# Attention and a feed-forward layer in one kernel: x buffers moved, weight copies issued later, a block's accumulators taken in another order

## The chip, the cores and the metric

The kernel runs on one core of a Trainium2 chip. A core has TensorE (PE in the profile, its weight loads PEld), VectorE (DVE), ScalarE (ACT), GpSimd (POOL), and SyncE (SP), which here only issues DMAs; 16 DMA engines move the data. The metric is the device time of one execution in microseconds, lower is better. Times of several runs are given as their median.

## The reference

Banded causal attention, then a feed-forward layer with a gate. All inputs and outputs are float32. Batch 8, 8 heads, 576 positions, head size 64; the feed-forward layer has 4608 tokens, width 512 and inner width 2048.

```python
scores = scale * np.matmul(q, k.transpose(0, 1, 3, 2))
rel = pos[:, None] - pos[None, :]
scores = np.where((rel >= 0) & (rel < 64), scores, -1000000000.0)
scores = scores - np.max(scores, axis=-1, keepdims=True)
attn = np.exp(scores)
attn = attn / (np.sum(attn, axis=-1, keepdims=True) + 1e-09)
x = np.matmul(attn, v)                       # to (4608, 512): tokens by heads x head size
h = x @ w_in
g = np.where(h >= 1, h, np.where(h <= -1, 0.0, (h + 1) ** 2 / 4.0))
return (g @ w_out).astype(np.float32)
```

## The kernel before, in words

**Precision.** Matrix products of the feed-forward layer are done in float32r, a form in which TensorE takes 32-bit operands. Each operand is split into a high part and the rest (`xh` and `xl` of x, `gh` and `gl` of the gate, two parts of each weight), and a product is three matmuls: high by high, high by rest, rest by high.

**Tiles.** The 4608 tokens are nine tiles of 512. The inner width is cut in 16 pieces f of 128. For the first three tiles ("plain", t = 0, 1, 2) `ffn_in` (L892) multiplies x by a piece of `w_in`, twelve matmuls of 512 columns (or two lots of 256 for the first pieces of tiles 0 and 1), the gate is worked out by ScalarE, VectorE and GpSimd (`ffn_relu`, `ffn_square`, `ffn_gate`, `ffn_high`, `ffn_low`, L906 to L933), and `ffn_out` (L938) multiplies it by a piece of `w_out` into four accumulators of one PSUM bank each, three matmuls for each 128 tokens. After the sixteenth piece `ffn_take` copies an accumulator to SBUF and `ffn_store` sends it to DRAM.

**Supers.** The other six tiles are three pairs, "supers" u = 0, 1, 2. A pair's first products are made by a scheme with seven products in place of eight: `add_products` (L857) and `ffn_product` (L824, matmuls at L831) take sums and differences of x (`x_op`, built by `add_build`) and sums and differences of weights. The moving operand of L831 is one of these x operands: some are stored in two buffers of the pool of x (called `xs` in the profile), the others in slots that weights had held (called `wts`). The halves of a super are its two tiles: `add_half(u, 0, ...)` runs the first, `add_half(u, 1, ...)` the second, each with its 16 gates and `ffn_out` (L950) into the same four accumulators, whose copies (`ffn_take`, at L274 or L276) free them.

**Weights.** They are loaded, decoded and split while tile 0 runs. Then `add_sums` (L781) prepares eight blocks of them for the supers: for block n, `sum_pass` (L739) copies three parts as they are to a DRAM buffer `kept` (three DMAs, L742), and for each half c `sum_whole` and `sum_sums` (L752 to L764) make sums in the small buffer `u`, `sum_high` and `sum_low` split them (the high parts go to a buffer of the pool `o`, which tile stores use too), and `sum_keep` (L774) stores both to `kept`. `ring_load` (L808) brings all parts back during the supers.

**Order.** Nothing is ordered by hand alone: `Plan` (L114) holds every piece of work with a key (its due place), costs by engine, what it comes after, and which buffers it takes and gives back. `run` simulates the engines with these costs and issues on each engine, among what could start soonest, the work with the lowest key; it also picks between engines where a piece may run on several. That order is then each engine's order on the chip, where instructions of one engine run strictly in order and wait only for the data and buffers that they need. What a piece "comes after" in the plan alone orders it and makes no wait on the chip. SP is one more engine of this plan, and all loads and stores but the first two are on its queue. The accumulators are the pool `acc` (4), the gate's parts `gh` and `gl` have two buffers each, `o` has two.

**Memory.** Pools lie behind one another in SBUF in the order of their opening: `const` (with `idt`, `msk`, `nmsk`, `idr`, `mskr`, `ptd`), `xpool` (x and its operands), `ld` (loads of q, k, v), `att` (`sm`, `nm`, `den`), `ffn` (`u`, `a`, `gh`, `gl`, `o`), `wpool` (weights).

Of the kernel before, what the change touches and what calls it, by code (L numbers as in the profile page):

```python
# [10 lines left out]
F32 = mybir.dt.float32  # L11
F32R = mybir.dt.float32r
# [8 lines left out]
P = 128  # L21
QB = 64
SB = 2 * QB
WIN = 128
WINDOW = 64
SQ = 32
NEAR = WINDOW + SQ
# [34 lines left out]
O_LAG_DMA = 2300  # L62
# [32 lines left out]
O_LATER = 1.5  # L95
# [11 lines left out]
SPILLED = 6  # L107
L_DVE = 4, 6, 8
G_LEAD = 1
H_LOAD = 1400  # L110
H_LEAD = 3.5


class Plan:  # L114
# [9 lines left out]
    def add(self, key, cost, do, after=(), takes=(), gives=(), lag=0, shared=False):  # L124
        self.work.append((key, cost, do, set(after), takes, gives, lag, shared))
        return len(self.work) - 1
# [75 lines left out]
def banded_attention_then_ffn(ctx: ExitStack, tc: tile.TileContext, q, k, v, w, masks, out, dims):  # L202
    nc = tc.nc
    B, H, S, D = dims
    NT, DM = out.shape
    NP = H // 2
# [3 lines left out]
    scale = 1.0 / float(D) ** 0.5  # L210
    TMAX = max(TILES)

    const = ctx.enter_context(tc.tile_pool(name="const", bufs=1))
    xpool = ctx.enter_context(tc.tile_pool(name="xpool", bufs=1))
    ld = ctx.enter_context(tc.tile_pool(name="ld", bufs=2))
    att = ctx.enter_context(tc.tile_pool(name="att", bufs=4))
# [12 lines left out]
    idt = const.tile([P, P], F32, name="idt")  # L229
    make_identity(nc, idt)  # L230
    msk = const.tile([P, 3, WIN], F32, name="msk")
    nmsk = const.tile([P, 3, WIN], F32, name="nmsk")
    idr = const.tile([P, P], F32R, name="idr")
    mskr = const.tile([P, 3, WIN], F32R, name="mskr")
    wpool = ctx.enter_context(tc.tile_pool(name="wpool", bufs=1))
    dram = ctx.enter_context(tc.tile_pool(name="dram", bufs=1, space=bass.MemoryType.DRAM))
    kept = [dram.tile([P, 7, 2, 2, P], F32, name=f"kept{n}") for n in range(NF // 2)]
# [3 lines left out]
    for n, at in ((P, QB), (QB, 0)):  # L241
# [4 lines left out]
            out=m, in_=m, compare_op=ALU.is_ge, fill=NEG, base=at - 1, pattern=[[1, WIN]], channel_multiplier=-1  # L246
        )
        nc.gpsimd.affine_select(
            out=m, in_=m, compare_op=ALU.is_ge, fill=NEG, base=WINDOW - at, pattern=[[-1, WIN]], channel_multiplier=1
# [19 lines left out]
    add = plan.add  # L269
# [127 lines left out]
        nc.sync.dma_start(out=t, in_=v[b * QB:b * QB + WIN])  # L397

    def load_masks():
        nc.sync.dma_start(out=nmsk[:, :, :NEAR], in_=masks)  # L400

    def round_masks():
        nc.scalar.copy(idr, idt)
        nc.scalar.mul(mskr[:, :2], msk[:, :2], 1.0 / scale)

    def att_scores(s, masked, pool):
        qt, kt = qts.pop(s), kts.pop(s)
        banks = [banks_of_heads(pool) for _ in range(2)]
        if masked:
            m = mskr[:, variant(s), :].unsqueeze(1).broadcast_to([P, NP, WIN])  # L410
            for ps in banks:
                nc.tensor.matmul(ps.rearrange("p a n -> p (a n)"), lhsT=idr, rhs=m, start=True, stop=False)
        m, n = (SQ, NEAR) if near(s) else (QB, WIN)
        for p in range(NP):
            for i in range(SB // m):
                r = slice(i * m, (i + 1) * m)
                for h in range(2):
                    nc.tensor.matmul(  # L418
                        banks[h][r, p, :n], lhsT=qt[half[h], p, r], rhs=kt[half[h], p, i * m:i * m + n],
                        start=not masked, stop=not masked or p == NP - 1,  # L420
                    )
        sm = att.tile([P, 2 * NP * WIN], F32, name="sm", bufs=BUFS["sm"])[:, :2 * NP * n]
        sm = sm.rearrange("p (h a n) -> p h a n", h=2, n=n)
        nm, den = (att.tile([P, 2, NP], F32, name=n, bufs=2) for n in ("nm", "den"))
        for h in range(2):
            blk[s, h] = banks[h][:, :, :n], sm[:, h], nm[:, h], den[:, h]
        blk[s, BOTH] = None, sm, nm, den
# [311 lines left out]
    def sum_pass(n):  # L739
        f0, f1 = by_chunk(n)  # L740
        for o, w_, e in (0, f0, 0), (5, f0, 1), (6, f1, 1):
            nc.sync.dma_start(  # L742
                out=kept[n][:, o].rearrange("p a c n -> p (a c) n"),
                in_=w_[:, :, :, e].bitcast(F32).rearrange("p a c n -> p (a c) n"),
            )
# [30 lines left out]
        nc.sync.dma_start(out=k[:, 1:5, 0, c], in_=half_of.pop((n, c)))  # L776
        nc.sync.dma_start(out=k[:, 1:5, 1, c], in_=sum_block(n, c))

    l1, sums_read, sums_kept, sum_last = {}, {}, {}, []

    def add_sums(n):  # L781
        key = step(1) + S_PACE * n + (S_LATE if n < 2 else S_LATER)
        ready = [w_ready[2 * n, 0], w_ready[2 * n + 1, 0], w_ready[NF - 1, 0], w_ready[NF - 1, 1]]
        xp = add(key, dict(SP=2000), lambda e: sum_pass(n), ready, lag=O_LAG_DMA)
        reads, keeps = [xp], [xp]
        for c in range(2):
            k = key + c * S_PACE / 2
            xs = add(
                k, tt(2 * P), lambda e, c=c: sum_whole(n, c, 0, e), ready + sum_last,
                takes=["tmp"] if sum_first else ["tmp", "u"], shared=True,  # L790
            )
            if not sum_first:
                sum_first.append(xs)
            x0 = add(k, tt(2 * P), lambda e, c=c: sum_whole(n, c, 1, e), [xs], shared=True)
            reads.append(x0)
            sum_last[:] = [xs]
            x = x0
            for j in range(4):
                x = add(k, tt(P), lambda e, c=c, j=j: sum_sums(n, c, j, e), [x], shared=True)
            xh = add(k, dict(ACT=90 + .84 * 4 * P), lambda e, c=c: sum_high(n, c, e), [x], takes=["o"])  # L800
            x = add(k, tt(4 * P), lambda e, c=c: sum_low(n, c, e), [xh], shared=True)
            x = add(k, dict(SP=750), lambda e, c=c: sum_keep(n, c), [x], lag=O_LAG_DMA, gives=[("tmp", xs), ("o", xh)])
            keeps.append(x)
        sums_read[n], sums_kept[n] = reads, keeps
# [219 lines left out]
    def add_stores(t, key, first, x_out):  # L1024
        end_tile, at_h, xh, sh = t == len(TILES) - 1, t >= PLAIN and (t - PLAIN) % 2 == 0, None, []
        for i in range(TILES[t] // P):
            pool = "sm" if end_tile and i < BUFS["sm"] else "hA1" if at_h and i > 1 else "o"
            xp, needs = xh if pool == "hA1" else None, [x_out[i]] + ([xh] if pool == "hA1" and xh else [])
            for n in pieces(t, i):
                m, end = n.stop - n.start, n.stop == DM  # L1030
                xo = add(
                    key + i * end_tile, dict(DVE=65 + m * 1.05, ACT=60 + m * .83), lambda e, i=i, n=n, pool=pool: ffn_take(t, i, n, e, pool),
                    needs, takes=[] if xp else [pool], gives=[("acc", *first[i])] * end,
                )
                xp = xo if xp is None else xp
                needs = [x_out[i], xo]
                xs = add(
                    key, dict(SP=790), lambda e, i=i, n=n: ffn_store(t, i, n), [xo, *sh], lag=O_LAG_DMA,
                    gives=[(pool, xp)] * (end and not (pool == "hA1" and i == 2)),
                )  # L1040
            if pool == "hA1":
                xh, sh = xp, [xs]
        return xh

    def add_ffn(t):
# [33 lines left out]
    def add_half(u, b, done, back):  # L1079
        t = PLAIN + 2 * u + b  # L1080
        r = slice(0, TILES[t])
        first, x_out, over = {}, {}, []
        for q in range(NF):
            f = (q + 2 * SPILLED * b) % NF
            n, e = f // 2, f % 2
            if b:
                key = step(PLAIN + 2 * u) + C_STEP * NF / 2 + Q_STEP * q
                key, lag = key - G_LEAD, O_LATER + G_LEAD
                split = Q_STEP / 4
            else:  # L1090
                key = step(t) + C_STEP * (n + (3 + 3 * e) / 7)
                lag = O_AFTER - C_STEP * (3 + 3 * e) / 7 + e * C_STEP / 2
                split = C_STEP / 8

            h_at[t, f] = int(back[n][e][0][2]), back[n][e][1]
            xa, xg, xh, xl = add_gate(
                t, f, r, key, [0] * 5, done[n][e], [(back[n][e][0], back[n][e][2])] * e, sup["relu"], sup["gate"]
            )
            sup["relu"], sup["gate"] = [xa], [xg]
            ends = q in (0, NF - 1)  # L1100
            groups = [(i,) for i in range(4)] if ends else [(0, 1), (2, 3)]
            for m, some in enumerate(groups):
                xo = add(
                    key + lag + split * some[0], dict(PE=3 * len(some) * 229), lambda e_, f=f, some=some: ffn_out(t, f, r, some),
                    [xl, w_ready[f, 1], *over], takes=[] if q else ["acc"] * len(some),
                    gives=[("gh", xh), ("gl", xl)] * (some[-1] == 3),
                )
                if q < NF - 1:
                    over = [xo]
                for k, i in enumerate(some):  # L1110
                    x_out[i] = xo
                    first.setdefault(i, (xo, k))
        return add_stores(t, key, first, x_out)
# [41 lines left out]
    a_keys, key = {}, float("inf")  # L1155
    for u in reversed(range(SUPERS)):
        end, apart = A_SUPER[u > 0]
        for i in reversed(A_ORDER):
            t = PLAIN + 2 * u
# [81 lines left out]
```

## Time and profile before

| | |
|---|---|
| median of 3 runs | 888.4 us (886.26 to 888.56) |
| the profiled execution | 887.9 us, its span 886.0 us |
| mean granted TensorE clock | 0.992 |
| TensorE busy | 866.9 us (98% of the span) |
| VectorE, ScalarE, GpSimd busy | 646.3, 499.4, 190.9 us |
| DMA | 147.57 MB, 167 GB/s over the span |

The span runs from the first to the last instruction; the time has 1.9 us around it. A row of the timeline or of the groups names the line, the engine, the operation, and the buffers as out<-in; a row of the waits has engine, buffer and line, then who ended the wait, the sum in us, how often, and the longest. Matmuls overlap one another, so the length of a row of matmuls reaches into the next one; from start to start of two rows is the time that the first really took. In the chain that ended last a row is a start, a length and what it was.

### The profile page before, as it was taken

What the parts mean: (1) busy time and instruction counts of PE and PEld (TensorE: products, weight loads), DVE (VectorE), ACT (ScalarE), POOL (GpSimd) and SP (SyncE); (2) the same over time, 40 slices, a digit from 0 to 9 for tenths busy, and PEclk for the clock granted to TensorE, in tenths of its full rate; (3) what the DMA queues carried; (4) which work ended last, traced back from release to release, by engine and by line L of the source; (5) the groups of instructions that cost most, each with busy time, mean ns of one, the idle gap of its engine ahead of it and who ended that gap; (6) DMA issues with size and microseconds to landing.
All of it is one profiled execution on the core that took longest, in us unless ns stands there. A gap on an engine that the chain in (4) does not pass through costs nothing.

```text
span 886.0 us, 17772 instructions
## 1 busy us (share of the span) xinstructions
PE 866.9 (98%) x6687; PEld 699.8 (79%) x6687; DVE 646.3 (73%) x1278; ACT 499.4 (56%) x1246; POOL 190.9 (22%) x202
## 2 busy tenths in 40 slices
PE   7899999999999999999999999999999999999998
PEld 5778887877777788877878788887887888888786
DVE  6999997888877776797888985587889633333443
ACT  6999965556464656545346864443548643333464
POOL 1000045554422352121113331111130011111000
PEclk8999999999999999999999999999999999999999
DMA  9992179445333313667666606676544045554221
GB/s 320 419 361 86 40 214 322 126 150 180 130 126 126 108 55 119 231 204 226 188 198 191 205 13 202 187 215 203 176 137 155 24 140 170 160 158 147 100 100 48
DMA packets 88372, 147.57 MB, mean 167 GB/s; under 512 B 7776, under 2 KB 36704, under 8 KB 88288
## 3 DMA queue, kind: packets, MB, share of 16 engines
q1 hardware_dynamic: 88000, 145.53, 50.9%
q8 instruction: 53, 0.87, 0.4%
q10 hardware_dynamic: 288, 0.92, 0.3%
q14 instruction: 31, 0.25, 0.1%
HBM read 112.86 MB, written 33.55 MB: 165 GB/s over the span
## 4 chain that ended last, share of the span: by engine, by line
PE 86%; DVE 6%; DMA 5%; ACT 2%; POOL 1%; issue 1%; ACTq 0%; DVEq 0%; POOLq 0%
PE acc L950 40%; PE ps_h L831 26%; PE ps_h L898 12%; PE ps_a L493 3%; PE ps_a L418 3%; DMA raw<-in_w 3%; DVE ptd L464 1%; DVE sm L458 1%; DMA kept<-u 1%; DVE a L923 1%; DMA out<-o 1%; ACT sm L446 1%; DMA kept<-o 1%; DVE gl L933 0%; DVE h L846 0%
## 5 line engine op out<-in xcount | busy, mean ns | idle before, releaser
L950 PE MATMUL acc<-wts,gh 128*128 128x512 f32 x1154 | 362.2, 395 | 2.1 <-ACT h L274 2.0
L950 PEld LDWEIGHTS acc<-wts,gh 128*128 128x128 f32 x1154 | 212.9, 188 | 51.5 <-ACT h L274 3.3
L950 PE MATMUL acc<-wts,gl 128*128 128x512 f32 x577 | 225.8, 391 | 1.4 <-DVE gl L933 0.8
L933 POOL TENSOR_TENSOR gl<-a,gh 128x512 fp32r<-128x512 f32 (+1 forms) x82 | 105.2, 1283 | 440.9 <-ACT gh L928 430.5
L831 PE MATMUL ps_h<-wts 128*128 128x512 f32 x720 | 179.1, 390 | 0.0
L831 PEld LDWEIGHTS ps_h<-wts 128*128 128x128 f32 x720 | 134.7, 188 | 28.7
L464 DVE STREAM_TRANSPOSE ptd<-sm 32x256 f32<-32x256 f32 x336 | 146.5, 436 | 6.3 <-PE ps_a L493 0.3
L846 DVE TENSOR_TENSOR h<-h,ps_h 128x512 f32<-128x512 f32 x120 | 82.2, 685 | 80.1 <-PE ps_h L831 79.0
L928 ACT CAST gh<-a 128x512 fp32r<-128x512 f32 (+1 forms) x149 | 89.5, 602 | 87.5 <-DVE a L923 79.4
L898 PE MATMUL ps_h<-xh,wts 128*128 128x512 f32 (+1 forms) x424 | 133.6, 382 | 4.6 <-DVE a L923 3.3
L950 PEld LDWEIGHTS acc<-wts,gl 128*128 128x128 f32 x577 | 108.4, 188 | 27.2 <-DVE gl L933 2.4
L911 ACT ACTIVATE a<-h 128x512 f32<-128x512 f32 x96 | 60.3, 631 | 101.2 <-DVE h L846 74.1
L923 DVE SCALAR_TENSOR_TENSOR a<-a,h 128x512 f32<-128x512 f32 x96 | 67.1, 700 | 65.5 <-ACT a L916 63.7
L446 ACT ACTIVATE sm<-sm,nm 128x96 f32<-128x96 f32 (+1 forms) x256 | 93.2, 366 | 19.0 <-DVE nm L439 19.0
L898 PEld LDWEIGHTS ps_h<-xh,wts 128*128 128x128 f32 x424 | 78.5, 191 | 21.5 <-DVE a L923 4.3
L916 ACT ACTIVATE a<-a 128x512 f32<-128x512 f32 (+1 forms) x136 | 83.8, 616 | 4.2
L898 PE MATMUL ps_h<-xl,wts 128*128 128x512 f32 (+1 forms) x212 | 80.0, 377 | 0.5 <-DVE xl L506 0.5
L831 PE MATMUL ps_h<-xs,wts 128*128 128x512 f32 x288 | 75.0, 395 | 0.0
L274 ACT COPY h<-ps_h 128x512 f32<-128x512 f32 x46 | 27.0, 587 | 74.4 <-PE ps_h L831 74.1
L831 PEld LDWEIGHTS ps_h<-xs,wts 128*128 128x128 f32 x288 | 53.7, 188 | 12.1
L911 ACT ACTIVATE a<-ps_h 128x512 f32<-128x512 f32 (+1 forms) x53 | 29.4, 554 | 42.1 <-PE ps_h L898 39.5
L933 DVE TENSOR_TENSOR gl<-a,gh 128x512 fp32r<-128x512 f32 (+1 forms) x67 | 44.7, 668 | 7.7 <-ACT gh L928 7.3
(106 smaller groups left out, 837.7 us busy)
## 6 DMA issues: line engine op xcount, KB each, us to landing
wts<-kept SPq DMA_DIRECT2D x168, 256.0 KB, 3.0
vt<-in_v SPq DMA_DIRECT2D x72, 256.0 KB, 3.6
kt<-in_k SPq DMA_DIRECT2D x35, 384.0 KB, 4.3
raw<-in_w SPq DMA_DIRECT2D x12, 1023.8 KB, 11.3
qt<-in_q SPq DMA_DIRECT2D x36, 256.0 KB, 3.1
spill<-h SPq DMA_DIRECT2D x18, 512.0 KB, 3.0
h<-spill SPq DMA_DIRECT2D x18, 512.0 KB, 3.7
out<-o SPq DMA_DIRECT2D x27, 256.0 KB, 2.5
```

Of the source, the lines that this page charges most:

```text
L274: nc.scalar.copy(dst, src)
L446: nc.scalar.activation(sm[:, p, :], (ps if masked else sm)[:, p, :], AF.Exp, bias=nm[:, p:p + 1], scale=scale if masked else 1.0, accum_ou ...
L464: nc.vector.transpose(dst[:, :, r], src[:, :, c * SQ:(c + 1) * SQ])
L831: nc.tensor.matmul(ps, lhsT=r[:, part, cp], rhs=x_op(k, xp)[:, cp], start=j in (0, 1, 3, 4) and i == 0 and cp == 0, stop=j in (1, 2, 5, 6) ...
L846: nc.vector.tensor_tensor(out=h[:, to], in0=h[:, of], in1=prods[u, n, b], op=ALU.add)
L898: nc.tensor.matmul(ps, lhsT=wts[f, 0][:, part, c * P:(c + 1) * P], rhs=x[:, c, r], start=(c == 0 and j == 0), stop=(c == NP - 1 and j == 2),)
L911: nc.scalar.activation(gs[t, f, r.start][0], phs[t, f, r.start], AF.Relu, bias=0.5, scale=0.5)
L916: nc.scalar.activation(a, a, AF.Square)
L923: nc.vector.scalar_tensor_tensor(out=a, in0=a, scalar=1.0, in1=ps, op0=ALU.min, op1=ALU.max)
L928: nc.scalar.copy(g[1], g[0])
L933: engine[eng].tensor_tensor(out=g[2], in0=g[0], in1=g[1].bitcast(F32), op=ALU.subtract)
L950: nc.tensor.matmul(acc[t, i][:, n], lhsT=g[:, sub], rhs=wts[f, 1][:, part, n], start=(q == 0 and j == 0), stop=(q == NF - 1 and j == 2 and ...
```

## The change

Three edits with no common code.

1. `nmsk` loses its unused columns (128 to 96 for each of three masks), `mskr` its unused third mask; the small tiles `nm` and `den` are allocated twice as long and used as before. All buffers behind them get other addresses.
2. In `add_sums` the copies of `sum_pass` no longer come first in a block. They come after the second half's `sum_whole` and, in the plan, after the copies of the block before; the first of them comes after the last store of tile 0, which `add_stores` notes in `sum_passed`. Readers of the copies (`sums_read`, `sums_kept`) still wait for them.
3. In `add_half`, the second half's first products (q = 0), those that take the four accumulators, get a lag that is longer by `B_LATER` = 2.6 steps of the plan.

```diff
+B_LATER = 2.6
...
-    nmsk = const.tile([P, 3, WIN], F32, name="nmsk")
+    nmsk = const.tile([P, 3, NEAR], F32, name="nmsk")
...
-    mskr = const.tile([P, 3, WIN], F32R, name="mskr")
+    mskr = const.tile([P, 2, WIN], F32R, name="mskr")
...
-        nm, den = (att.tile([P, 2, NP], F32, name=n, bufs=2) for n in ("nm", "den"))
+        nm, den = (att.tile([P, 4, NP], F32, name=n, bufs=2)[:, :2] for n in ("nm", "den"))
...
-    l1, sums_read, sums_kept, sum_last = {}, {}, {}, []
+    l1, sums_read, sums_kept, sum_last, sum_passed = {}, {}, {}, [], []
...
-        xp = add(key, dict(SP=2000), lambda e: sum_pass(n), ready, lag=O_LAG_DMA)
-        reads, keeps = [xp], [xp]
+        reads, keeps = [], []
...
             x0 = add(k, tt(2 * P), lambda e, c=c: sum_whole(n, c, 1, e), [xs], shared=True)
             reads.append(x0)
+            if c:
+                sum_passed[:] = [add(k, dict(SP=2000), lambda e: sum_pass(n), [x0, *sum_passed], lag=O_LAG_DMA)]
+                reads += sum_passed
+                keeps += sum_passed
...
+        if t == 0:
+            sum_passed[:] = [xs]
         return xh
...
                 key = step(PLAIN + 2 * u) + C_STEP * NF / 2 + Q_STEP * q
-                key, lag = key - G_LEAD, O_LATER + G_LEAD
+                key, lag = key - G_LEAD, O_LATER + G_LEAD + B_LATER * (q == 0)
```

More of the change, by code (lines that the diff above doesn't have):

```diff
@@ L399, in load_masks @@
     def load_masks():
-        nc.sync.dma_start(out=nmsk[:, :, :NEAR], in_=masks)
+        nc.sync.dma_start(out=nmsk, in_=masks)
     def round_masks():
         nc.scalar.copy(idr, idt)
-        nc.scalar.mul(mskr[:, :2], msk[:, :2], 1.0 / scale)
+        nc.scalar.mul(mskr, msk[:, :2], 1.0 / scale)
     def att_scores(s, masked, pool):
```

## The prediction, made before the result was known

> **What bounds the kernel now.** I read the page first, then the busy time by stage, then what TensorE waited for, and last the single rows of its idle places.
>
> ```profile
> PE 866.9 (98%) x6687; PEld 699.8 (79%) x6687; DVE 646.3 (73%) x1278; ACT 499.4 (56%) x1246; POOL 190.9 (22%) x202
> ...
> PE 86%; DVE 6%; DMA 5%; ACT 2%; POOL 1%; issue 1%; ACTq 0%; DVEq 0%; POOLq 0%
> ```
>
> TensorE is busy for 866.9 of 886.0 us and holds 86% of the chain that ended last. So time comes off in two ways only: its idle places close, or its matmuls follow one another faster.
>
> Stage, its length, then busy us of PE, PEld, DVE, ACT and POOL with counts, the granted clock, the DMA share and GB/s:
>
> ```profile
> 22.00:113.00 91.00, 87.24 (x684) 71.66 (x679) 88.37 (x172) 86.11 (x182) 0.00 (x0) 0.98 0.57 221
> 113.00:152.00 39.00, 36.99 (x292) 30.65 (x291) 32.84 (x75) 23.60 (x66) 20.90 (x30) 0.96 0.96 294
> 152.00:215.00 63.00, 62.27 (x614) 49.50 (x613) 54.92 (x113) 33.93 (x94) 35.62 (x40) 1.00 0.50 150
> ```
>
> From 22 to 113 us VectorE (88.37 of 91 us) limits as much as TensorE does: a faster matmul is worth little there. From 113 to 152 us the DMA engines are 96% busy, TensorE idles 2 us and its granted clock falls to 0.96. From 152 us on TensorE alone is the limit.
>
> ```profile
> PE ps_h L898 <- DVE a L923: 3.3, 3, 2.0
> PE acc L950 <- ACT h L274: 2.0, 3, 0.7
> ```
>
> The longest wait of the first row and the three waits of the second are what parts 2 and 3 of the change can reach.
>
> **Part 1, addresses.** In the program of before, the buffers of x start at byte 13,952 of a partition, which is 54 x 256 + 128; the slots of the weights start at 98,048 = 383 x 256. The change takes 384 bytes from `nmsk` and 512 from `mskr`, both ahead of x: x moves to 13,056 = 51 x 256. Four small tiles behind x grow by 32 bytes each, so the weights move by 768, to 380 x 256. No instruction is added. L831 shows what the address is worth, because it runs the same loop with its moving operand in an x buffer (`xs`) or in a weight slot (`wts`). Timeline of TensorE, start and length in us:
>
> ```profile
> 803.43 1.55 PE L831 MATMUL ps_h<-xs,wts 128*128 128x512 f32 x6
> 804.82 0.63 PE L950 MATMUL acc<-wts,gh 128*128 128x512 f32 x2
> ...
> 806.20 1.52 PE L831 MATMUL ps_h<-wts 128*128 128x512 f32 x6
> 807.56 0.62 PE L950 MATMUL acc<-wts,gh 128*128 128x512 f32 x2
> ...
> 808.92 1.52 PE L831 MATMUL ps_h<-wts 128*128 128x512 f32 x6
> ...
> 813.05 2.88 PE L831 MATMUL ps_h<-wts 128*128 128x512 f32 x12
> 815.77 0.62 PE L950 MATMUL acc<-wts,gh 128*128 128x512 f32 x2
> ...
> 330.91 0.40 PE L898 MATMUL ps_h<-xh,wts 128*128 128x512 f32 x1
> ...
> 333.70 0.63 PE L950 MATMUL acc<-wts,gh 128*128 128x512 f32 x2
> ...
> 340.49 0.63 PE L950 MATMUL acc<-wts,gh 128*128 128x512 f32 x2
> ...
> 341.19 0.62 PE L950 MATMUL acc<-wts,gh 128*128 128x512 f32 x2
> ```
>
> Six matmuls on `xs` take 804.82 - 803.43 = 1.39 us from start to start, six on `wts` 807.56 - 806.20 = 1.36. With the six L950 matmuls that follow it is 2.77 against 2.72 (803.43, 806.20, 808.92): the slower rhythm lasts a little beyond its cause. L898, whose moving operand is always an x buffer, takes 2.79 for twelve (330.91 to 333.70) against 2.72 for twelve on weight slots (813.05 to 815.77); behind it a triple of L950 takes 0.70 (340.49 to 341.19), not 0.68 (half of 807.56 to 808.92). The counts:
>
> ```profile
> L898 PE MATMUL ps_h<-xh,wts 128*128 128x512 f32 x344 | 116.9, 401 | 2.3 <-DVE a L923 2.3
> L831 PE MATMUL ps_h<-xs,wts 128*128 128x512 f32 x288 | 75.0, 395 | 0.0
> L898 PE MATMUL ps_h<-xl,wts 128*128 128x512 f32 x172 | 68.2, 396 | 0.0
> ```
>
> 288 / 6 = 48 groups on `xs` at 0.05 are 2.4 us. (344 + 172) / 12 = 43 groups of L898 at 0.07 are 3.0 us. Behind each of these 43 come twelve of L950, of which some run at 0.70 per triple and some at 0.68: up to 0.08 a group, half of it taken, 1.7 us. That makes 7.1. Thirteen of the 43 are tile 0's (its first three products are split in halves of 256 columns), nearly all ahead of 113 us, where VectorE limits as well; I count them out, 13 x 0.11 = 1.4, and take **-5.7 us**. The ends are 0 (128 against 0 past a multiple of 256 isn't the cause; the rows only show that the place of the buffer is) and -8.8 (the full 0.08, nothing counted out). A loss isn't excluded, since the weight slots move too, by 768 bytes; but both places are multiples of 256, and I leave it to the tail.
>
> Trainium skill, "SBUF — State Buffer", section "Specifications (TRN2)": SBUF is read in lines of 16 bytes, and two hits in a line give full bandwidth. By that rule a contiguous row at 128 bytes past a multiple of 256 is as good as any, and this part would be worth nothing. The rows above, 1.39 against 1.36 us in one loop, speak against it; it is a rival below.
>
> **Part 2, the weight copies.** `sum_pass` issues three DMAs for each of eight blocks, 24 of L742. They now go on SP's queue behind the last store of tile 0, and then each behind the sums that read the same block. Before, they stood in front. SP's queue, the DMA issues, and the chain:
>
> ```profile
> 128.88 3.77 SPq L742 DMA_DIRECT2D kept<-wts  x6
> ...
> 135.45 1.77 SPq L742 DMA_DIRECT2D kept<-wts  x3
> 137.32 1.84 SPq L980 DMA_DIRECT2D out<-o  x2
> ```
> ```profile
> out<-o SPq DMA_DIRECT2D x27, 256.0 KB, 2.5
> ```
> ```profile
> 132.75 4.57 DMA kept<-o
> 137.32 6.04 DMA out<-o
> ...
> 143.45 0.69 DVE o L276
> ...
> 146.34 4.21 PE ps_h L898 x12
> 150.56 1.79 PE acc L950 x6
> 152.34 2.81 PE ps_h L898 x12
> ```
> ```profile
> 146.34 0.50 PE L898 MATMUL ps_h<-xh,wts 128*128 128x512 f32 x1 [2.01 <-DVE a L923]
> ```
>
> Nine copies were issued in the 8.4 us ahead of the first two stores of tile 0. Those took 6.04 us to land instead of the median 2.5, VectorE's copy into the same buffer stood until 143.45, and the gate that TensorE needs is behind it in VectorE's order. TensorE idled 2.01 us and was then at half rate for some matmuls: 4.21 - 2.81 for the twelve and 1.79 - 1.36 for six are 1.8 us. Together **-3.8 us**. With stores landing in 2.5 us, 3.5 us earlier, the buffer is free before VectorE comes to it, so I count the stall out whole. The other end is 0: something else holds VectorE as long.
>
> The copies don't vanish. 24 x 256 KB = 6.3 MB go into the stage of 63 us that moved 150 GB/s at a DMA share of 0.50: some 100 GB/s more, so the engines don't saturate, but a landing can be queued. SP waits for nothing new, since the copies read weights that are long finished; behind each triple stand the loads of q, k, v and the stores `kept<-u`, on which the sums wait:
>
> ```profile
> POOL u L755 <- DMA kept<-u: 4.7, 3, 3.6
> ...
> DVE u L755 <- DMA kept<-u: 3.4, 2, 2.5
> ```
>
> These are 8.1 us of waits now, nearly all hidden. I take **+1.0 us** for more of them showing through, between 0 and 3.8 (one more stall like that of 146.34).
>
> **Part 3, accumulators.** In each of three blocks of two tiles ("supers") the second half's first products take the four accumulators of the first half. By the planner's keys, relative to the block's start, the first half's last four groups stand at 31.7 to 33.1 (11/3 x 7.86 + 4.2 - 3.14 + 1.83, plus 0.46 for each next) and the second half's first four at 30.8 to 31.5 (29.33 + 1.5, plus 0.21). So the planner lets three of the second half pass ahead of the first half's last, and the fourth then meets an accumulator that was only just finished. With 2.6 more they stand at 33.4 to 34.1, behind all.
>
> ```profile
> 488.99 0.39 PE L950 MATMUL acc<-wts,gl 128*128 128x512 f32 x1
> 489.42 0.58 ACT L274 COPY h<-acc 128x512 f32<-128x512 f32 x1 [0.94 <-PE acc L950]
> 490.06 0.73 PE L950 MATMUL acc<-wts,gh 128*128 128x512 f32 x2 [0.68 <-ACT h L274]
> ...
> 674.75 0.73 PE L950 MATMUL acc<-wts,gh 128*128 128x512 f32 x2 [0.68 <-ACT h L274]
> ...
> 676.71 0.50 PE L950 MATMUL acc<-wts,gl 128*128 128x512 f32 x1 [0.53 <-DVE gl L933]
> ...
> 840.50 0.73 PE L950 MATMUL acc<-wts,gh 128*128 128x512 f32 x2 [0.68 <-ACT h L274]
> ```
>
> From 488.99 to 490.06 is 1.07 us where a matmul's pitch is 0.23: 0.84 lost, and the same 0.68 of idle stands in each block, so 2.5 us. Afterwards the four copies out of PSUM (0.58 each) run one triple (0.68) apart, and the second half's group i comes four triples, 2.7 us, after the first half's group i: its copy is covered by three triples of other work. Next in line is the gate's product `gl`: 676.71 waits 0.53 for it, and that chain stood behind the same late copy on ScalarE; I take half, 0.3. Together **-2.8 us**, between 0 (other work of the plan takes the place) and -3.2.
>
> **The sum** against the profiled execution's own 887.9 us (span 886.0): -5.7 - 3.8 + 1.0 - 2.8 = -11.3. The plan is worked out anew after the first changed cost, so the order of VectorE, ScalarE and GpSimd shifts over 750 us; I add 1.0 for one new wait of the size seen above (0.5 to 0.8), between -1 and +4. That gives 877.6; the median of before, 888.4, lies 0.5 higher: 878.1, say **878 us**.
>
> **The rivals.**
> *Addresses do nothing* (chance 0.15). For it: no row has an x buffer at another address. Against it: one loop, two paces, by buffer alone. 878 + 5.7 = 884. The lines of 16 bytes that the Trainium skill states (above) are the mechanism that would give this.
> *The copies only move their stall* (0.14): `kept<-u` lands late once where VectorE is 87% busy (54.92 of 63 us). 878 + 3.8 = 882.
> *The order stays* (0.06): the planner finds the old order, or another stall of 0.8 at each block's middle. 878 + 2.8 = 881.
> *Slower* (0.07): the copies, now between the sums, delay `kept<-u` in most of eight blocks; VectorE and GpSimd stand in order behind L755, `gl` and the gate come late, TensorE idles 2.0 us and drops to half rate each time, 3.8 us. It decides from the third such stall on (878 + 3 x 3.8 = 889); with four it is 893. For it: 3.6 us was the longest such wait already. Against it: only five waits, 8.1 us, in the whole trace, and a DMA share of 0.50.
>
> **How the numbers follow.** My forecast has 0.58, with a range of its own of 873 to 882. The low end of the whole range is 872: addresses at -8.8, no price for the copies, and the new plan gaining 1.0 (878 - 3.1 - 1.0 - 2.0); the high end takes in the first three rivals: 886. About 0.3% (2.7 us) is what a measurement of this kernel tells from no change, so faster means under 885.7: 0.58 + 0.14 + 0.06 and most of the first rival make 0.87; within 0.3% 0.07; slower 0.06.
>
> **What would show it.** Right: `xs` and `wts` groups of L831 both at 1.36 us per six and L898 at 2.72 per twelve; the first stores of tile 0 landing in under 3.5 us and no TensorE row with 2 us of idle near 145; no wait of L950 for a copy L274 at the middle of a block. Wrong: L898 still at 2.79 (rival one); PEclk under 1.00 between 152 and 215 us with waits for `kept<-u` above 8.1 us (rivals two and four); new waits at other places, which would show that the re-made plan, which I priced at 1.0, weighs more.

## The result, and the profile after

The changed kernel takes 877.74 us (median of 5 runs, 875.81 to 878.39) against 888.4 us before (886.26 to 888.56): a ratio of 0.9883, 95% interval 0.9866 to 0.9899. Timed again later beside other kernels it gave 0.9873 (0.986 to 0.9886). Two single runs far above all others, 1066.21 us of the kernel before and 1714.58 us of the one with a lag of 1.0, are left out of the comparisons. The ratios rest on all other runs, so they can differ by some hundredths of a per cent from the ratio of two medians. The forecast was 878, and the direction and size are right. The profiled execution has a span of 876.1 us, 9.9 less than before. The busy time over the span, then by stage (stage, length, busy us of PE, PEld, DVE, ACT, POOL with counts, granted clock, DMA share, GB/s):

```profile
PE 861.0 (98%) x6687; PEld 700.1 (80%) x6687; DVE 643.0 (73%) x1272; ACT 494.9 (56%) x1239; POOL 197.8 (23%) x215
```
```profile
113.00:150.00 37.00, 36.93 (x299) 30.94 (x298) 33.86 (x76) 23.69 (x67) 22.03 (x30) 1.00 0.52 165
150.00:213.00 63.00, 61.50 (x607) 49.32 (x606) 53.28 (x107) 33.73 (x96) 36.87 (x43) 0.97 0.70 209
```

The same matmuls are there (6687). From 113 to 150 us TensorE no longer idles, its granted clock is 1.00, and the DMA share is 0.52, not 0.96. From 150 to 213 us it idles 1.5 us (0.7 before, from 152 to 215), and its clock fell to 0.97; this is looked at below. (The line numbers of the changed kernel are higher by up to 4: L835 is L831, L902 is L898, L954 is L950.)

The rhythm of the matmuls, in TensorE's timeline:

```profile
794.84 1.52 PE L835 MATMUL ps_h<-xs,wts 128*128 128x512 f32 x6
796.20 0.62 PE L954 MATMUL acc<-wts,gh 128*128 128x512 f32 x2
...
797.56 1.52 PE L835 MATMUL ps_h<-wts 128*128 128x512 f32 x6
798.92 0.62 PE L954 MATMUL acc<-wts,gh 128*128 128x512 f32 x2
```
```profile
326.62 0.39 PE L902 MATMUL ps_h<-xh,wts 128*128 128x512 f32 x1
...
329.35 0.61 PE L954 MATMUL acc<-wts,gh 128*128 128x512 f32 x2
...
330.02 0.61 PE L954 MATMUL acc<-wts,gh 128*128 128x512 f32 x2
```

Six on `xs` take 796.20 - 794.84 = 1.36 us, as six on `wts` (797.56 to 798.92). Twelve of L902 take 2.73 (326.62 to 329.35), not 2.79, and a triple of L954 behind them 0.67, not 0.70.

SP's queue and the places where the stores of tile 0 stand now, then VectorE's copy into the buffer that the first of them frees, before and after:

```profile
135.48 1.57 SPq L984 DMA_DIRECT2D out<-o  x2
...
140.50 1.44 SPq L984 DMA_DIRECT2D out<-o  x2
141.99 1.69 SPq L743 DMA_DIRECT2D kept<-wts  x3
```
```profile
143.45 0.69 DVE L276 COPY o<-acc 128x512 f32<-128x512 f32 x1 [3.48 <-DMA out<-o]
```
```profile
139.78 0.69 DVE L277 COPY o<-acc 128x512 f32<-128x512 f32 x1 [0.35 <-DMA out<-o]
```

All four stores are out before the first weight copy, and VectorE waits 0.35 us for the first of them, not 3.48. That store landed 4.2 us after its issue, against 6.0 before, and it was issued 1.84 us earlier (135.48 against 137.32). The long wait of L898 for the gate is gone; what is left of it:

```profile
PE ps_h L902 <- DVE a L927: 0.9, 1, 0.9
```

The wait for L274 (the copy out of an accumulator, now L275) doesn't appear any more. At the middle of the first super:

```profile
480.33 1.28 ACT L275 COPY o<-acc 128x512 f32<-128x512 f32 x2
...
481.71 1.27 ACT L275 COPY h<-acc 128x512 f32<-128x512 f32 x2
...
483.33 0.39 PE L954 MATMUL acc<-wts,gl 128*128 128x512 f32 x1
483.56 0.61 PE L954 MATMUL acc<-wts,gh 128*128 128x512 f32 x2
```

The four copies run one behind the other, and TensorE goes on at 0.23 us a matmul.

### The profile page after: what moved, and what is told of

It is laid out like the page before. It is cut to its first block, busy times and chain, and to the rows that moved or that the text cites. A ratio compares the mean times of both kernels' runs of the same rounds, so it can differ in the third digit from the quotient of the medians.

```text
span 876.1 us, 17766 instructions
## 1 busy us (share of the span) xinstructions
PE 861.0 (98%) x6687; PEld 700.1 (80%) x6687; DVE 643.0 (73%) x1272; ACT 494.9 (56%) x1239; POOL 197.8 (23%) x215
## 4 chain that ended last, share of the span: by engine, by line
PE 90%; DVE 3%; DMA 2%; ACT 1%; POOL 1%; issue 1%; ACTq 0%; SPq 0%; POOLq 0%; DVEq 0%
PE acc L954 43%; PE ps_h L835 26%; PE ps_h L902 13%; PE ps_a L494 3%; PE ps_a L419 3%; DMA kept<-u 1%; DMA vt<-in_v 1%; DMA raw<-in_w 1%; DVE ptd L465 0%; DVE a L927 0%; POOL gl L937 0%; DVE sm L459 0%; ACT sm L447 0%; PE acc L494 0%; PE ps_h L480 0%
## 5 line engine op out<-in xcount | busy, mean ns | idle before, releaser
L954 PE MATMUL acc<-wts,gh 128*128 128x512 f32 x1154 | 362.2, 395 | 0.9 <-ACT gh L932 0.9
L954 PEld LDWEIGHTS acc<-wts,gh 128*128 128x128 f32 x1154 | 213.3, 188 | 48.2 <-ACT gh L932 1.5
L954 PE MATMUL acc<-wts,gl 128*128 128x512 f32 x577 | 225.8, 391 | 1.5 <-POOL gl L937 1.0
L835 PE MATMUL ps_h<-wts 128*128 128x512 f32 x720 | 179.0, 390 | 0.0
L835 PEld LDWEIGHTS ps_h<-wts 128*128 128x128 f32 x720 | 134.7, 188 | 28.6
L902 PE MATMUL ps_h<-xh,wts 128*128 128x512 f32 (+1 forms) x424 | 130.1, 374 | 1.9 <-DVE a L927 0.9
L954 PEld LDWEIGHTS acc<-wts,gl 128*128 128x128 f32 x577 | 108.7, 188 | 26.3 <-POOL gl L937 1.9
L902 PEld LDWEIGHTS ps_h<-xh,wts 128*128 128x128 f32 x424 | 77.5, 188 | 17.0 <-DVE a L927 1.6
L920 ACT ACTIVATE a<-a 128x512 f32<-128x512 f32 (+1 forms) x130 | 80.0, 616 | 4.1
L902 PE MATMUL ps_h<-xl,wts 128*128 128x512 f32 (+1 forms) x212 | 78.5, 370 | 0.7 <-DVE xl L507 0.7
L835 PE MATMUL ps_h<-xs,wts 128*128 128x512 f32 x288 | 73.5, 390 | 0.0
L275 ACT COPY h<-ps_h 128x512 f32<-128x512 f32 x47 | 27.5, 586 | 73.6 <-PE ps_h L835 73.1
L835 PEld LDWEIGHTS ps_h<-xs,wts 128*128 128x128 f32 x288 | 53.8, 188 | 11.4
L447 ACT ACTIVATION_READ_ACCUMULATOR sm<-sm,nm 128x1 f32 x256 | 48.3, 189 | 0.0
## 6 DMA issues: line engine op xcount, KB each, us to landing
raw<-in_w SPq DMA_DIRECT2D x12, 1023.8 KB, 10.1
```

The source lines that it names most:

```text
L275: nc.scalar.copy(dst, src)
L447: nc.scalar.activation(sm[:, p, :], (ps if masked else sm)[:, p, :], AF.Exp, bias=nm[:, p:p + 1], scale=scale if masked else 1.0, accum_ou ...
L835: nc.tensor.matmul(ps, lhsT=r[:, part, cp], rhs=x_op(k, xp)[:, cp], start=j in (0, 1, 3, 4) and i == 0 and cp == 0, stop=j in (1, 2, 5, 6) ...
L902: nc.tensor.matmul(ps, lhsT=wts[f, 0][:, part, c * P:(c + 1) * P], rhs=x[:, c, r], start=(c == 0 and j == 0), stop=(c == NP - 1 and j == 2),)
L920: nc.scalar.activation(a, a, AF.Square)
L954: nc.tensor.matmul(acc[t, i][:, n], lhsT=g[:, sub], rhs=wts[f, 1][:, part, n], start=(q == 0 and j == 0), stop=(q == NF - 1 and j == 2 and ...
```

## The experiments

All are compared with the kernel before, timed on the same chip; the percentages below are differences of such ratios, and 0.1% is 0.89 us.

| kernel | median us | ratio to before | 95% interval |
|---|---|---|---|
| changed kernel, again | 875.82 | 0.9873 | 0.986 to 0.9886 |
| part 1 alone (addresses) | 881.14 | 0.994 | 0.9926 to 0.9953 |
| part 2 alone (copies) | 883.82 | 0.9971 | 0.9957 to 0.9985 |
| part 3 alone (accumulators) | 884.26 | 0.9967 | 0.9956 to 0.9977 |
| changed, x at 64 | 880.99 | 0.9933 | 0.992 to 0.9946 |
| changed, weights at 128 | 888.23 | 1.0015 | 1.0006 to 1.0024 |
| changed, gates at 128 | 883.82 | 0.9966 | 0.9953 to 0.9979 |
| changed, all at 128 | 875.95 | 0.9882 | 0.9869 to 0.9895 |
| changed, copies last | 876.56 | 0.988 | 0.9867 to 0.9892 |
| changed, lag 1.0 | 879.83 | 0.9927 | 0.9913 to 0.9941 |

### One part of the change at a time

**Part 1 alone** (the lines of `nmsk`, `mskr`, `nm`, `den`).

> Part 1 of the change alone: the x buffers at a multiple of 256 bytes, the weight slots moved from one multiple of 256 to another, the plan of before. My theory (the place of the moving operand sets the rhythm of the matmuls): six L831 matmuls on xs go from 1.39 to 1.36 us, twelve of L898 from 2.79 to 2.72, and the time falls by 4 to 6 us, to about 883.5. Rival (the place is nothing, other causes brought the whole gain): within 1 us of before, L898 still at 2.79.

-0.60%, 5.3 us (4.2 to 6.6). TensorE's timeline:

```profile
799.80 1.52 PE L831 MATMUL ps_h<-xs,wts 128*128 128x512 f32 x6
801.16 0.61 PE L950 MATMUL acc<-wts,gh 128*128 128x512 f32 x2
```
```profile
329.09 0.39 PE L898 MATMUL ps_h<-xh,wts 128*128 128x512 f32 x1
...
331.81 0.62 PE L950 MATMUL acc<-wts,gh 128*128 128x512 f32 x2
```

1.36 and 2.72: both rhythms are changed by the addresses alone. The plan is that of before, so no other cause is in it. The stall behind tile 0's stores is still there, and it is as long as before, but what follows differs:

```profile
147.59 0.50 PE L898 MATMUL ps_h<-xh,wts 128*128 128x512 f32 x1 [2.02 <-DVE a L923]
...
150.46 0.61 PE L950 MATMUL acc<-wts,gh 128*128 128x512 f32 x2
```

The twelve matmuls behind the idle time take 2.87 us here (147.59 to 150.46). Before, with 2.01 us of idle, they took 4.01 (146.34 to 150.35, where the next L950 starts). So the half rate that the prediction counted in part 2, 1.8 us, doesn't follow each time on this stall.

**Part 2 alone** (the lines of `sum_pass` and `sum_passed`).

> Part 2 alone: the weight copies behind tile 0's last store and between the sums. The 2.01 us of idle near 146 and the half rate behind it go (-3.8 us). What the changed kernel's trace shows near 184 (idle of 0.88 and 0.62 us, then seven matmuls at half rate, some 3.2 us lost against about 1.1 before) comes back here if the copies cause it: -1.7 us in all, about 886.7. Rival (that stall belongs to the other two parts or to the new plan): no half rate near 184, -2.8 to -3.8 us, 884.6 to 885.6.

-0.29%, 2.6 us, between the two expectations, and the interval (1.3 to 3.8) holds both. TensorE's wait for the gate, then the waits of the two engines that make the sums, then TensorE near 184 us:

```profile
PE ps_h L901 <- DVE a L926: 0.9, 1, 0.9
```
```profile
POOL u L755 <- DMA kept<-u: 9.2, 3, 5.2
...
DVE u L755 <- DMA kept<-u: 2.7, 1, 2.7
```
```profile
186.26 0.50 PE L953 MATMUL acc<-wts,gl 128*128 128x512 f32 x1 [0.63 <-POOL gl L936]
186.60 0.62 PE L953 MATMUL acc<-wts,gh 128*128 128x512 f32 x2
```

Of the three waits of L898 for the gate (3.3 us) one of 0.9 is left. Near 184 us there is 0.63 us of idle and no half rate (the row of two takes 0.62 us, 1.05 at half rate), as the rival said. The waits for `kept<-u` are 11.9 us in all, against 8.1 before, and the growth is on GpSimd. It is not told from the spread, though: part 1 alone, with the copies where they were, has 10.1, and the two profiles of the changed kernel have 8.6 and 12.5. TensorE lost nothing by it that the rows show.

**Part 3 alone** (`B_LATER`).

> Part 3 alone: the longer lag of the second half's first products. My theory: the three waits of L950 for L274 (0.68 us idle each) and the wait of 0.53 us for gl behind the second of them go, and the time falls by 2 to 3 us, to about 885.8. Rival (the loss only moves to the next wait, for gl): waits for gl of 0.3 to 0.6 us at the middle of each block take half of it back, -1 us or less.

-0.33%, 2.9 us (2.0 to 3.9): my theory's number. In its waits the copy out of an accumulator, L274, is gone. The waits for `gl` are 1.0 us in all (1.4 before), and at the middle of a block none is over 0.3.

The stall behind tile 0's stores, which this kernel keeps, came out longer here than before, without anything changed at it:

```profile
146.03 0.50 PE L899 MATMUL ps_h<-xh,wts 128*128 128x512 f32 x1 [2.94 <-DVE a L924]
```

The three parts give 0.60 + 0.29 + 0.33 = 1.22%; together they gave 1.17 and 1.27%. Within their intervals they add up; no loss of one to another is seen.

### What an address must be

**x at 64 past a multiple of 256.**

```diff
-    nmsk = const.tile([P, 3, NEAR], F32, name="nmsk")
+    nmsk = const.tile([P, 3 * NEAR + 16], F32, name="nmsk")[:, :3 * NEAR].rearrange("p (a n) -> p a n", a=3)
...
-        nm, den = (att.tile([P, 4, NP], F32, name=n, bufs=2)[:, :2] for n in ("nm", "den"))
+        nm, den = (att.tile([P, m, NP], F32, name=n, bufs=2)[:, :2] for n, m in (("nm", 4), ("den", 2)))
```

> The changed kernel with the x buffers, the loads of q, k, v and sm moved on by 64 bytes, to 64 past a multiple of 256; the weight slots stay at a multiple of 256. If what counts is the remainder to 256, the pitch of L902 and of L835 on xs is slow again: 4 to 6 us more than the changed kernel, about 882.5, with twelve L902 at 2.79 or more. Rival (only the old place or only 128 past a multiple is bad; an address at 64 is as good as one at 0): 877.7.

0.60% slower than the changed kernel beside it, 5.3 us: the whole of part 1 is lost.

```profile
797.05 1.55 PE L835 MATMUL ps_h<-xs,wts 128*128 128x512 f32 x6
798.44 0.63 PE L954 MATMUL acc<-wts,gh 128*128 128x512 f32 x2
```

1.39 again, so for L835 on `xs` 64 is as bad as 128. L902 suffers less: twelve take 2.76 (325.65 to 328.41), between 2.72 and 2.79. Over the whole run its matmuls on `xh` have a mean of 397 ns (394 in the changed kernel, 401 before), and those on `xl` have the changed kernel's 390 (396 before):

```profile
L902 PE MATMUL ps_h<-xh,wts 128*128 128x512 f32 x344 | 115.3, 397 | 0.1
L902 PE MATMUL ps_h<-xl,wts 128*128 128x512 f32 x172 | 67.1, 390 | 0.0
```

**Weights at 128.** x stays; the tiles `o` ahead of the weight slots are 64 bytes longer.

```diff
-                o = ffn.tile([P, DM], F32, name="o", bufs=BUFS["o"])
+                o = ffn.tile([P, DM + 16], F32, name="o", bufs=BUFS["o"])[:, :DM]
```

(The same for the other use of that tile.)

> The changed kernel with the weight slots moved on by 128 bytes (through longer o tiles) and x left at a multiple of 256. The weight slots hold the moving operand of all L954 matmuls and of the L835 ones on wts, and the stationary operand of L902 and L835. If a moving operand at 128 past a multiple of 256 costs 5 ns a matmul, 1731 + 720 of them cost about 12 us: 890. If the stationary operand counts too, L902 and L835 on xs are slow as well: up to 4 us more. Rival (something of the old x buffers other than the remainder to 256): 877.7.

1.42% slower than the changed kernel, 12.6 us, all of what was gained and a little more. The number fits the first line of the expectation, but the rows don't:

```profile
793.43 1.52 PE L835 MATMUL ps_h<-wts 128*128 128x512 f32 x6
794.79 1.55 PE L835 MATMUL ps_h<-xs,wts 128*128 128x512 f32 x6
796.18 0.63 PE L954 MATMUL acc<-wts,gh 128*128 128x512 f32 x2
...
796.88 0.63 PE L954 MATMUL acc<-wts,gh 128*128 128x512 f32 x2
```

Six on `wts`, whose moving operand is now at 128, take 794.79 - 793.43 = 1.36, the fast rhythm. Six on `xs`, whose moving operand is at 0, take 1.39, the slow one. L954 takes 0.70 a triple. What is fast has both operands at 128 (the stationary operand of L835 is in a weight slot); what is slow has one at 0 and one at 128. My theory (A), a multiple of 256 for the moving operand, falls here. The new one (B): the two operands must have the same remainder to 256. Two kernels tell them apart.

**All at 128**: `nmsk` is 128 bytes longer, and everything behind it moves.

```diff
-    nmsk = const.tile([P, 3, NEAR], F32, name="nmsk")
+    nmsk = const.tile([P, 3 * NEAR + 32], F32, name="nmsk")[:, :3 * NEAR].rearrange("p (a n) -> p a n", a=3)
```

> The changed kernel with everything behind nmsk moved on by 128 bytes: x, the gate's parts and the weight slots all stand at 128 past a multiple of 256. Theory A (the moving operand must start at a multiple of 256): all large matmuls are slow, 3300 of them at 5 ns, about +15 us, 892. Theory B (moving and stationary operand must have the same remainder to 256; the weights at 128 beside weights at 128 already ran at nearly full pace in the run before, with x at 0 beside them slow): 877.7, every pitch at 0.227.

0.9882, as the changed kernel: no large operand stands at a multiple of 256, and nothing is lost.

```profile
793.80 1.52 PE L835 MATMUL ps_h<-xs,wts 128*128 128x512 f32 x6
795.16 0.61 PE L954 MATMUL acc<-wts,gh 128*128 128x512 f32 x2
```

**Gates at 128**: only the stationary operand of L954 moves (the tiles `a` ahead of `gh` and `gl` are longer by 64 bytes each, `o` too, so that the weights end at a multiple of 256).

```diff
-        return ffn.tile([P, TMAX], dt, name=name, bufs=BUFS[name])[:, :r.stop - r.start]
+        return ffn.tile([P, TMAX + 16 * (name == "a")], dt, name=name, bufs=BUFS[name])[:, :r.stop - r.start]
```

> The changed kernel with the gate's parts gh and gl, the stationary operand of L954, at 128 past a multiple of 256; x and the weight slots stay at multiples of 256. Theory A (only the moving operand's place counts): 877.7. Theory B (the two operands' remainders must agree): the 1731 matmuls of L954 run at 0.232 in place of 0.227, about +9 us, 886.5, and L902 and L835 hardly change.

0.9966: 0.83 to 0.93% slower than the changed kernel in its two timings, 7.4 to 8.2 us, where theory A has no loss. Matmuls whose moving operand didn't move at all are slow:

```profile
799.04 1.53 PE L835 MATMUL ps_h<-xs,wts 128*128 128x512 f32 x6
800.41 0.64 PE L954 MATMUL acc<-wts,gh 128*128 128x512 f32 x2
...
801.11 0.62 PE L954 MATMUL acc<-wts,gh 128*128 128x512 f32 x2
```

L954 takes 0.70 a triple; L835 on `xs`, whose operands agree, 1.37. The means over the whole run say the same, with all at 128 and then with the gates at 128:

```profile
L954 PE MATMUL acc<-wts,gh 128*128 128x512 f32 x1150 | 360.2, 394 | 0.1
```
```profile
L954 PE MATMUL acc<-wts,gh 128*128 128x512 f32 x1150 | 365.7, 399 | 0.5 <-ACT gh L932 0.5
```

So the remainders to 256 of the moving and the stationary operand must agree. Over the six layouts here every group with both at 0 or both at 128 is fast, and every group with 0 and 128 or 128 and 0 is slow. At 64 and 0 all groups are slow but one, L902 on `xl`, and that one is not explained. No other remainder was tried, nor a pair at 64 and 64. Why the pair counts is not shown. The weight loads (PEld, busy for 80% of the span) run beside the matmuls (98%), so a conflict between the two reads would fit; it is argued only.

### Are the moved copies to blame for the stall near 184 us?

In the changed kernel's profile TensorE idled twice and then ran at half rate (0.43 us from 187.36 to 187.79 for a matmul); in the second execution that was profiled it idled too, but the rhythm held:

```profile
184.87 0.73 PE L954 MATMUL acc<-wts,gh 128*128 128x512 f32 x2 [0.88 <-ACT gh L932]
186.22 0.50 PE L954 MATMUL acc<-wts,gl 128*128 128x512 f32 x1 [0.62 <-POOL gl L937]
...
187.36 0.63 PE L954 MATMUL acc<-wts,gl 128*128 128x512 f32 x1
187.79 1.05 PE L954 MATMUL acc<-wts,gh 128*128 128x512 f32 x2
```
```profile
184.12 0.73 PE L954 MATMUL acc<-wts,gh 128*128 128x512 f32 x2 [0.42 <-ACT gh L932]
185.47 0.50 PE L954 MATMUL acc<-wts,gl 128*128 128x512 f32 x1 [0.62 <-POOL gl L937]
185.81 0.62 PE L954 MATMUL acc<-wts,gh 128*128 128x512 f32 x2
```

The repetition:

> The changed kernel once more, beside the next three on one chip: 877.7 us within a us.

It took 875.82 us, 1.9 less than the 877.7 and so outside the us that I had allowed. Against the kernel before, timed beside each, the two ratios (0.9883 and 0.9873) agree within their intervals.

**Copies last**: all 24 behind the last sum.

```diff
-            if c:
-                sum_passed[:] = [add(k, dict(SP=2000), lambda e: sum_pass(n), [x0, *sum_passed], lag=O_LAG_DMA)]
-                reads += sum_passed
-                keeps += sum_passed
...
         sums_read[n], sums_kept[n] = reads, keeps
+        if n == NF // 2 - 1:
+            for m in range(NF // 2):
+                sum_passed[:] = [add(key, dict(SP=2000), lambda e, m=m: sum_pass(m), [x0, *sum_passed], lag=O_LAG_DMA)]
+                sums_read[m] += sum_passed
+                sums_kept[m] += sum_passed
```

> The changed kernel with all 24 weight copies behind the last sum of block 8, so that none lies among the sums. If the copies between the sums cause the stall near 184, it shrinks to what it was before the change (1.1 us in place of 3.2, no half rate) and the time falls by 2 us against the changed kernel, to about 875.6. Rival (the transfer kept<-u of the sums is slow by its neighbours, the loads of q, k and v, whatever the copies do): the wait of VectorE for kept<-u near 180 stays over 3 us, and the time stays within 1 us of the changed kernel; a second rival: the copies, now in one lump after 205 us, delay the loads and stores there and cost a new stall of 2 to 4 us.

0.988 against 0.9873 beside it: no gain, 0.6 us the other way, within both intervals. The chain of waits of the kernel before, of the changed kernel, then of this one:

```profile
178.82 4.83 DMA kept<-u
```
```profile
174.08 5.73 DMA kept<-u
...
183.57 0.61 DVE a L927
```
```profile
174.10 4.52 DMA kept<-u
...
182.38 0.61 DVE a L928
```

Without any copy among the sums the transfer `kept<-u` still takes 4.52 us, and VectorE stands for it for 2.2 us (3.4 and 2.9 in the two profiles of the changed kernel). The gate comes at 182.38, 1.2 us earlier than the 183.57 of the changed kernel's first profile and 0.4 earlier than the 182.82 of its second. The other kernels settle more: before the change, and with part 1 or part 3 alone, no weight copy is issued after 150 us, and this landing took 4.83, 5.36 and 5.29 us; with the copies moved it took 5.73 and 5.29 (the changed kernel twice) and 5.06 (part 2 alone). The two ranges overlap, so no delay by the copies is shown. The idle time of TensorE near 184 us doesn't need them either: it is 1.1 us with part 1 alone (0.47 and 0.62), 1.5 and 1.0 in the two profiles of the changed kernel, and 0.6 with part 2 alone. So the stall belongs to the place, and the first rival holds, though VectorE's wait of 2.2 us is under the 3 that it named. TensorE got nothing in the end; in this profile it has two waits further on (0.48 us for the gate at 223.93, 0.62 us at 254.30) that neither profile of the changed kernel has, and whether the remade order brought them is not shown.

What keeps `kept<-u` slow at this one place stays open.

### How much lag the accumulators need

```diff
-B_LATER = 2.6
+B_LATER = 1.0
```

> The changed kernel with the added lag at 1.0 steps in place of 2.6. By the planner's keys the second half's first four groups then stand at 31.8 to 32.5, still ahead of the first half's third and fourth (32.6 and 33.1). Theory: only when all four of the first half end first is the wait gone, so the three waits for L274 of 0.68 us come back, +2 to +2.5 us, 880. Rival (any delay is enough, the gain came from the remade order): 877.7.

0.9927, 0.44 to 0.54% slower than the changed kernel in its two timings: the wait is back as it was.

```profile
PE acc L954 <- ACT h L275: 2.0, 3, 0.7
```

So a delay that, by the keys, leaves the second half's groups ahead of the first half's last two doesn't help. The three waits with what hangs on them are 2.5 us by the prediction's working; the times say 3.9 to 4.8, and the nearest ends of the intervals are 1.2 and 2.4 us apart. The rest is not accounted for.

## Why the prediction was right or wrong

**Part 1, -5.7 us: 5.3 measured, right in size, wrong in its reason.** The step "128 against 0 past a multiple of 256" named the x buffers' remainder alone. The runs show that it is the pair that counts: with all at 128 nothing is lost, and with only the gates moved 1731 matmuls are slow that had not been. That the number came out was luck in this: the change happened to bring x to the remainder of the weights. My remark that the weight slots' own move by 768 bytes could be left to the tail was right only because 768 is a multiple of 256, as is the distance of x and weights after the change. The rival *addresses do nothing* is refuted: 64 bytes off costs the whole gain. Its mechanism, the lines of 16 bytes in "SBUF — State Buffer", "Specifications (TRN2)", of the Trainium skill, gives nothing for 64 bytes, which are four such lines; the measured 5.3 us decide. With the first thirteen groups counted out 5.7 stands against 5.3 (4.2 to 6.6), and the 7.1 of all groups would lie outside; how much of it each step of the sum brought was not measured.

**Part 2, -3.8 + 1.0: 2.6 measured against 2.8.** The path is as told: stores first, VectorE's wait for the buffer 0.35 us in place of 3.48, no idle near 145, a granted clock of 1.00 from 113 to 150 us. Two steps on it were wrong or unsure. The stores did not land in 2.5 us, nor in the "under 3.5" that was to be the sign, but in 4.2 and 3.7; that was enough because they were also issued 1.84 us earlier. And the stall's price isn't a constant, which the prediction didn't say: the idle time is 2.01 us before, 2.02 with part 1 alone and 2.94 with part 3 alone, and the half rate behind it, 1.8 of the 3.8 us, is missing with part 1 alone. So 2.6 may be 3.8 less a price of the moved copies, or a stall without half rate and no price; the runs don't tell these apart, and that the two terms together came near is in part luck. I had named a clock under 1.00 between 152 and 215 us with waits for `kept<-u` above 8.1 us as the mark of rivals two and four; both were there in the first profile (0.97 and 8.6), but the experiments don't lay them to the copies, and the second profile has the idle time without the slow matmuls. As a mark it was badly chosen, since a stall had been in that place before (0.62 us of idle for `gl` at 190.07).

**Part 3, -2.8: 2.9 measured.** The rows fit the order that the keys give: the three waits (0.84 us lost at each) are gone, and 1.0 of lag, which by the same keys isn't enough, brings them back. The 0.3 taken for `gl` is not shown in the whole change: the wait of 0.53 behind the second block's copy is gone, but `gl` is waited for 1.5 us in all, against 1.4 before.

**The remade plan, +1.0: neither shown nor excluded.** The three parts add up to what the whole gives, 1.22% against 1.17 and 1.27, but parts 2 and 3 each have a new plan of their own, so this sum can't show its price. Without the term the forecast is 877.1, which the measurements of 877.7 and 875.8 don't tell from 878.1. The waits that TensorE's timeline names after 42 us say a little more. They are 5.75 us in all before, of which 4.58 were to go (2.01, three times 0.68, 0.53), so 1.17 should be left; the two profiles of the changed kernel have 2.41 and 1.88. So new waits of 0.7 to 1.2 us came in, where the two terms of +1.0 had allowed 2.0.

**The rival on the other side** (copies delaying `kept<-u` in most blocks) did not come. The waits for it were 11.9 us with part 2 alone and 8.6 and 12.5 in the changed kernel, against 8.1 before and 10.1 with part 1 alone, and no stall beyond the one near 184 us, which was there before, followed from them in TensorE's rows. That most of these waits are GpSimd's, off the path, would explain it; this is argued.

## What to carry to other kernels

Where one loop runs at two paces, group its rows by the buffers that they read: a difference of 0.03 us in six matmuls led to 5 us of the kernel. Put the two operands of such float32r matmuls at the same remainder to 256 bytes, and look at it again when any tile ahead of them changes its size. Where accumulators change hands between two stages, let all of the first stage end before the second takes its first, if there is enough work in a group to cover the copy. An idle place in one profile is a sample: its length and the half rate behind it change from one execution to the next, so its price needs a range.

## What the hardware showed that I had not expected

Two operands of a matmul at remainders to 256 bytes that differ by 128 make each float32r matmul of 512 columns about 5 ns slower (0.232 against 0.227 us, 0.70 against 0.68 a triple), whichever of the two is moved. A difference of 64 costs L835 on `xs` the same (1.39 for six), L902 less (2.76 for twelve against 2.79). The slow rhythm lasts into matmuls whose operands agree, for several of them: a triple of L950 behind L898 took 0.70 before and 0.67 in the changed kernel, though the distance of its own two operands was the same.

After some idle times of TensorE its matmuls run at 0.43 us in place of 0.23 for seven or eight matmuls, after others of the same length they don't: 2.01 us of idle before the change were followed by it, 2.02 at the same place with part 1 alone were not; 0.88 and 0.62 us within 1.4 us were, 0.42 and 0.62 at the same place were not.
